# A long convolution with a gated block: late projections in the following second-stage stretch, taps from SBUF, ScalarE evacuating the last third stage, 120-row input tiles, warm-up matmuls

## The chip, the cores and the metric

One core of one Trainium2 chip runs the whole kernel. The metric is the device time of one execution in microseconds (us). Five engines work side by side: TensorE (PE, matmuls; its weight loads are listed as PEld), VectorE (DVE), ScalarE (ACT), GpSimd (POOL) and SyncE (SP), which here only issues the DMAs between HBM and SBUF. An instruction of one engine runs when those ahead of it on the same engine have run and the data and buffers that it names are ready.

## The reference

For every batch and channel, x is convolved causally with h over the whole sequence (a real FFT of twice the length), and the result y goes through a gated block. All is float32.

```python
B, S, D = 8, 6400, 128                       # x; h is [S, D]
y = irfft(rfft(x, n=2*S) * rfft(h, n=2*S))[:, :S, :]
gate = sigmoid(sum(conv_w[k] * shift(y, 4 - k) for k in range(5)))   # 5 taps along S
out = ((y @ w_val) * gate) @ w_out           # both weights 128 x 128
```

## The kernel before, in words

**Four stages.** The convolution of length 6400 is a transform written as matmuls with 6400 = 100 x 64. *First stage* (`Forward`): for each of 16 groups of 4 channels an x tile of 128 rows (two halves of 64 rows, 50 of each used) is loaded, POOL or DVE forms its sum and difference (`sums`, tile `sd`), 16 matmuls go into a pair of PSUM banks (`half`), and ScalarE copies the result into the large tile `gy`. *Second stage* (`s2_mm`): 13 blocks of 4 frequencies; each block is 16 matmuls with weights from a table `m2`, and a `Product` multiplies it by the spectrum of h: DVE reads PSUM twice (`mul_u` into `gy`, `mul_t` into the spectrum's own tile, named `h`), then POOL combines the two (`add`). *Third stage* (`s3_quads`, L330): 16 groups a batch, each into two PSUM banks, which ScalarE (`e[0]`) and VectorE (`e[1]`, L591) copy into the tile `dt`. *Fourth stage* (`Chunk.s4`): 13 chunks of up to five 100-long rows, with weights from `dt` and a table `m4_sb`.

**What follows a chunk.** `copies`: ScalarE copies the chunk's y from PSUM into SBUF and forms one or two scaled copies for the taps. `taps`: VectorE adds the others with scalar_tensor_tensor operations (`more`), which read y from PSUM, `self.p`; POOL adds one more. `project` is two matmuls of y with `w_val` into a PSUM bank, `sigm` the sigmoid on ScalarE, `gate` VectorE's product of the two, `output` two matmuls with `w_out`, `store` ScalarE's copy and SP's DMA to `out`. One projection or output takes one of four single banks (`ps1`), as a fourth stage and each bank of a third-stage group do. First-stage halves and products take pairs of banks (`ps2`, two pairs).

**Order of the work.** All instructions keep program order on their engine; each is recorded under one line (L98), that of the wrapper. The chunk with the sequence's last rows (`HEAD`, 4 rows at 60) is needed first, since the rows of one chunk continue in the next. Each of 8 batches has two parts. In the *third stage* the loop over `g` (L584) runs one third-stage group and one half of the next batch's first stage. In the *stretch* the loop over `s` (L611) runs the fourth stage of this batch's chunk `s` and the product `s + 1` of the next batch. Chunk `s - 2` is projected in step `s`, gated in the same step, and its output stands in step `s + 1`, behind the next Product, the next chunk's projection and the next fourth stage. Chunks that begin at row 35 or later (five of them, `late`) and `HEAD` are treated otherwise: their y stays in tiles `yl`, their gates in `gl`, and a list of steps (`trail`, L538) runs their taps, projection, sigmoid, gate, output and store inside the next batch's third stage, one step after each group. Their taps read the SBUF copy already. In the last batch nothing is late, and there is no next batch: its stretch holds only fourth stages and what follows a chunk (`finish`, L562).

**The start.** A *head* runs the first stage for h and for batch 0, and then (L513) the second stage for both: for each block the spectrum of h, its copy and its store to DRAM (`hd`), and batch 0's product. DVE also unpacks the block's float64 weights to float32 by 22 operations on bits (`weights`, L140), two in each of these steps. The fourth-stage table is loaded in 13 DMAs (L596) in batch 0's third stage, since its space holds other tiles before.

Of the kernel before, what the change touches and what calls it, by code (L numbers as in the profile page):

```python
# [16 lines left out]
C = 128  # L17
# [4 lines left out]
HP = 64  # L22
MW = 3 * HR
SB = 4
# [86 lines left out]
def longconv_moe(ctx: ExitStack, tc: tile.TileContext, x, h, r1, m2, r3, m4, w64, out):  # L111
# [98 lines left out]
    class Forward:  # L210
# [6 lines left out]
        def load(self, n=1):  # L217
            for _ in range(n):
                if self.n < NS:
                    nc.sync.dma_start(self.xs[self.n % len(self.xs)], self.src[self.n])  # L220
                    self.n += 1

        def sums(self, e):
            j = self.s
            if j >= NS:
                return
            self.s += 1
            x, sd = self.xs[j % len(self.xs)], sd_sb[(j + self.o) % 3]
# [141 lines left out]
    class Chunk:  # L370
# [33 lines left out]
        def copies(self):  # L404
            a, n = self.ch
            if a == HEAD[0]:
# [6 lines left out]
                return  # L413
            if self.late:
                act(self.y, self.p)
                self.p = self.y
                return
            self.init()
            act(self.y, self.p)
            self.q = p_t[a // CH % 2]  # L420
            self.first(3, self.q, self.p)
# [57 lines left out]
        def store(self):  # L479
            act(self.y, self.o)  # L480
            i, k = _out_range(self.ch)
            nc.sync.dma_start(out[self.b, i:k].rearrange("(e n t) -> e n t", e=C, n=self.ch[1]), self.y)
# [12 lines left out]
    nc.sync.dma_start(r1_sb, r1)  # L495
    fh.load(len(xh) - 1)
# [14 lines left out]
    nc.sync.dma_start(r3_sb, r3)  # L511
    sp, pr = {0: Spectrum(0)}, {}
    for kb in range(-1, NKB + 1):  # L513
# [8 lines left out]
        if 0 <= kb < NKB:  # L522
# [3 lines left out]
            next(wgen, None)  # L526
            next(wgen, None)
# [4 lines left out]
    class Gates:  # L532


        def __init__(self, b, defer):
            self.cs = [Chunk(b, ch, defer) for ch in CHUNKS]

        def trail(self):  # L538

            h, late = self.cs[0], [c for c in self.cs if c.late]  # L540
            steps = collections.defaultdict(list)
            for m, c in enumerate(late + [h]):
                t = 2 * m + 2
                if c is not h:
                    steps[t - 2].append(lambda c=c: c.taps(range(2)))
                    steps[t - 1].append(lambda c=c: c.taps(range(2, 4)))
                steps[t] += [c.project, c.sigm, c.gate]
                steps[t + 2].append(c.output)
                steps[t + 3].append(c.store)
            n = max(steps)  # L550
            return [lambda c=steps[i]: [f() for f in c] for i in range(n + 1)]

        def at(self, s, last):

            return self.cs[s] if 1 <= s < NCH else self.cs[0] if s == NCH and last else None

        def each(self, what, s, last=True):
            c = self.at(s, last)
            if c and not c.late:
                getattr(c, what)()  # L560

        def finish(self, s):  # L562
            self.each("project", s - 2)
            self.each("output", s - 3)
            self.each("store", s - 4)
            self.each("sigm", s - 2)
            if s == NCH:
                self.cs[NCH - 1].taps()
            self.each("gate", s - 2)

    trail = []
    fx = Forward(x[1], gy) if B > 1 else None
    if fx:
        fx.load(XB)
    for b in range(B):
# [3 lines left out]
        if trail:  # L579
            trail.pop(0)()  # L580
# [3 lines left out]
        for g in range(NS):  # L584
# [6 lines left out]
            e[1](dve)  # L591
            for u in f:
                u(act)
            if b == 0 and g < NKB:
                a = CH * g
                nc.sync.dma_start(m4_sb[:, a : a + CH], m4.rearrange("k (n t) -> k n t", t=MW)[:, a : a + CH])  # L596
# [6 lines left out]
            if trail:  # L603
                trail.pop(0)()
# [4 lines left out]
        gs = Gates(b, nxt)  # L609
        ps = {}  # L610
        for s in range(NCH):  # L611
            if s == 0:
                gs.cs[0].s4()
                gs.cs[0].copies()
                if nxt:
                    ps[0] = Product(0)
                    m2_load(M2B)
            if s == 1:
                gs.cs[s].s4()
# [3 lines left out]
            gs.each("project", s - 2)  # L623
            if s > 1:
                gs.cs[s].s4()
            gs.each("output", s - 3)
            gs.each("store", s - 4)
            gs.each("sigm", s - 2)
            if s:
                gs.cs[s].copies()  # L630
            if nxt:
                ps[s].mul_u()
            if s > 1 and not gs.cs[s - 1].late:
                gs.cs[s - 1].taps()
            if nxt:
                ps[s].mul_t()
                ps.pop(s).add()
                h_load(s + HB)
            if s == 0:
                gs.cs[0].taps()  # L640
            gs.each("gate", s - 2)
            if s == 10 and b + 2 < B:
                fx.load(XB)
        trail = gs.trail() if nxt else [lambda s=s: gs.finish(s) for s in range(NCH, NCH + 5)]
    for t in trail:
        t()
# [45 lines left out]
```

## Time and profile before

| | us |
|---|---|
| median of 3 runs (lowest to highest) | 1005.45 (1003.25 to 1007.77) |
| the profiled execution | 1006.82 |
| its span in the profile | 1005.0 |
| PE busy | 940.5 (94% of the span) |
| DVE busy | 702.8 (70%) |
| POOL busy | 544.5 (54%) |
| ACT busy | 475.5 (47%) |

The profile is of one execution; its times are read against its own 1006.82 us, of which the span is 1005.0. Busy time of PE is that of its matmuls, whose records overlap a little: where matmuls follow each other without a hole, the time from one start to the next is the price. In a row of a timeline stand the start, the duration, the engine, the line, the operation, what it writes and reads, its shape and the count; a bracket at the end is the time for which the engine had been idle, and what released it. `dt`, `yl` and `gl` with `w_sb` are projections and outputs, `gy` with `m` is a Product, `m_sb` with `dt` a fourth stage, `r_sb` with `gy` a third-stage group and `r_sb` with `sd` a first-stage half.

### The profile page before, as it was taken

How to read it: one execution, taken by the hardware profiler on the slowest of the kernel's cores; microseconds unless marked ns; L12 is line 12 of the kernel's file. 1: busy time of each engine (PE TensorE's matmuls, PEld its weight loads, DVE VectorE, ACT ScalarE, POOL GpSimd, SP SyncE). 2: the span in 40 equal slices, each digit the busy share in tenths (PEclk: the TensorE clock that was granted, in tenths of full speed). 3: DMA queues.
4: the chain of work that ended last, by engine and by line, in shares of the span. 5: the costliest groups of instructions: out<-in, count | busy, mean ns of one | idle time of the engine just before them, and what ended most of it. 6: DMA issues, size and time to landing. Idle time of an engine off the chain costs nothing.

```text
span 1005.0 us, 46982 instructions
## 1 busy us (share of the span) xinstructions
PE 940.5 (94%) x21360; PEld 793.5 (79%) x21360; DVE 702.8 (70%) x939; ACT 475.5 (47%) x916; POOL 544.5 (54%) x551
## 2 busy tenths in 40 slices
PE   7897778999999999999999998999989999999987
PEld 7797778787978878887878778887887878786753
DVE  5499217977398747977398756977399755978366
ACT  4521434445543653546444554445544553534465
POOL 6467434785277744785177743784367752760032
PEclk9898999999999999999999999999999999999989
DMA  7783854756467545755467555665467554750012
GB/s 253 244 272 149 283 204 158 225 157 194 134 229 214 156 154 194 230 159 166 150 223 218 153 159 186 216 176 170 145 211 221 151 178 159 229 140 34 31 42 91
DMA packets 96838, 177.33 MB, mean 176 GB/s; under 512 B 43392, under 2 KB 49792, under 8 KB 96640
## 3 DMA queue, kind: packets, MB, share of 16 engines
q1 hardware_dynamic: 96640, 174.34, 55.6%
q8 instruction: 167, 2.74, 1.1%
q14 instruction: 31, 0.25, 0.1%
HBM read 141.55 MB, written 32.77 MB: 173 GB/s over the span
## 4 chain that ended last, share of the span: by engine, by line
PE 90%; issue 5%; DVE 3%; POOL 1%; ACT 1%; DMA 0%; POOLq 0%; DVEq 0%; ACTq 0%
PE pt L98 90%; DVE gl L98 1%; DVE dt L98 1%; POOL gl L98 1%; ACT dt L98 1%; DVE gy L98 0%; POOL dt L98 0%; DMA x<-hl 0%; DVE sd L98 0%; DVE m_sb L98 0%; POOLq L688 0%; ACT gl L98 0%; ACT yl L98 0%; ACT gy L98 0%; DVEq L98 0%
## 5 line engine op out<-in xcount | busy, mean ns | idle before, releaser
L98 PE MATMUL pt<-r_sb,gy 64*64 64x128 f32 (+1 forms) x8192 | 267.3, 273 | 20.3 <-issue 11.5
L98 PEld LDWEIGHTS pt<-r_sb,gy 64*64 64x64 f32 (+1 forms) x8192 | 235.8, 130 | 63.8 <-ACT gl L98 20.4
L98 POOL TENSOR_TENSOR sd<-x 128x256 f32<-128x256 f32 x236 | 197.4, 860 | 154.2 <-issue 124.2
L98 POOL TENSOR_TENSOR gy<-gy,h 128x512 f32<-128x512 f32 (+1 forms) x182 | 221.6, 1241 | 63.6 <-DVE h L98 27.7
L98 ACT COPY dt<-pt 128x512 f32<-128x512 f32 (+3 forms) x269 | 155.2, 581 | 193.9 <-PE pt L98 191.6
L98 PEld LDWEIGHTS pt<-m_sb,dt 128*64 128x64 f32 x4096 | 191.5, 137 | 35.3 <-issue 22.7
L98 PEld LDWEIGHTS pt<-gy,m 128*64 128x64 f32 x3008 | 179.1, 135 | 43.8 <-issue 23.6
L98 PE MATMUL pt<-gy,m 128*64 128x128 f32 x3008 | 193.3, 278 | 17.5 <-issue 12.0
L98 PE MATMUL pt<-m_sb,dt 128*64 128x100 f32 x4096 | 198.0, 250 | 2.9 <-DVE dt L98 2.4
L98 DVE COPY dt<-pt 128x512 f32<-128x512 f32 (+1 forms) x136 | 92.5, 680 | 132.1 <-PE pt L98 125.6
L98 PE MATMUL pt<-r_sb,sd 50*64 50x100 f32 x4608 | 143.2, 258 | 17.2 <-issue 11.2
L98 DVE TENSOR_TENSOR gy<-pt,h 128x1024 f32<-128x1024 f32 (+1 forms) x99 | 116.8, 1180 | 46.3 <-PE pt L98 46.3
L98 DVE SCALAR_TENSOR_TENSOR gl<-yl,w_sb,gl 128x500 f32<-128x500 f32 x147 | 130.6, 892 | 24.6 <-ACT gl L98 22.1
L98 PEld LDWEIGHTS pt<-r_sb,sd 50*64 50x64 f32 x4608 | 128.9, 142 | 22.2 <-issue 14.5
L98 DVE SCALAR_TENSOR_TENSOR dt<-pt,w_sb,dt 128x500 f32<-128x500 f32 (+7 forms) x216 | 132.9, 631 | 13.5 <-POOL dt L98 3.8
L98 ACT COPY gy<-pt 128x400 f32<-128x400 f32 x248 | 110.2, 496 | 41.2 <-PE pt L98 32.8
L98 ACT ACTIVATE dt<-pt,w_sb 128x500 f32<-128x500 f32 (+1 forms) x64 | 40.0, 625 | 170.2 <-PE pt L98 169.4
L98 PE MATMUL pt<-dt,w_sb 128*64 128x500 f32 (+2 forms) x480 | 116.0, 561 | 0.8 <-DVE dt L98 0.4
L98 POOL TENSOR_TENSOR dt<-dt,p 128x500 f32<-128x500 f32 (+1 forms) x64 | 66.4, 1038 | 82.5 <-DVE dt L98 58.0
L98 DVE TENSOR_TENSOR h<-pt,h 128x1024 f32<-128x1024 f32 (+1 forms) x91 | 107.3, 1179 | 2.3
L98 ACT COPY yl<-pt 128x500 f32<-128x500 f32 (+1 forms) x96 | 54.5, 568 | 83.9 <-PE pt L98 83.9
L98 DVE TENSOR_TENSOR gl<-pt,gl 128x500 f32<-128x500 f32 (+1 forms) x48 | 31.7, 661 | 54.5 <-PE pt L98 50.8
(40 smaller groups left out, 568.5 us busy)
## 6 DMA issues: line engine op xcount, KB each, us to landing
m<-m SPq DMA_DIRECT2D x90, 512.0 KB, 4.7
h<-hd SPq DMA_DIRECT2D x84, 512.0 KB, 3.9
x<-xl SPq DMA_DIRECT2D x118, 256.0 KB, 3.4
out<-dt SPq DMA_DIRECT2D x56, 250.0 KB, 5.8
out<-yl SPq DMA_DIRECT2D x40, 250.0 KB, 2.5
m_sb<-m SPq DMA_DIRECT2D x13, 375.0 KB, 4.5
hd<-h SPq DMA_DIRECT2D x8, 512.0 KB, 5.1
m_sb<-m SPq DMA_DIRECT2D x6, 512.0 KB, 6.5
```

What stands on the lines that cost most here:

```text
L98: return self._tc.keep_in_program_order(call(*args, **kwargs))
```

## The change

1. **Late projections.** The list of steps is gone. In the third stage stay only the ten half-sets of late taps and two sigmoids. Projection, gate, output and store of `HEAD` and of the five late chunks (`pend`) go into the stretch that follows, in its steps 0, 0, 1, 1, 2 and 3 (`jobs`). A chunk of the batch's own is projected one step later than before (`i + 3`), and its output is the first PE work of the step after (`outs`), right behind its projection.
2. **Order on VectorE.** In a step `mul_u`, `mul_t`, the gate and the taps of the previous chunk follow each other; before it was `mul_u`, taps, `mul_t`, gate.
3. **Taps** read the SBUF copy of y in every chunk (`self.p = self.y`).
4. **Last third stage.** In the last batch ScalarE evacuates both banks of a group.
5. **Input tiles.** Loads, sums and differences cover 120 rows instead of 128 (`XR`).
6. **Warm-up.** VectorE zeroes a 128 x 128 tile, and seven matmuls of it run ahead of the first stage.
7. **The start's other work.** The weight unpacking moves from the head into batch 0's third stage, two operations a group; four of the 13 loads of the fourth-stage table move from there into steps 0 to 3 of the head's second stage.

*First place.* PE's order in two steps of batch 0's stretch, before. Names with `m4_sb` are fourth stages, those with `m2` Products; `dt` with `w_sb` is, behind a Product, the projection, and behind a fourth stage the output of the chunk before.

```order
L98 MATMUL pt1_2603<-m4_sb_68,dt_67 64x2x50 x20
L98 MATMUL pt1_2624<-dt_67,w_sb_71 64x500 x2
L98 MATMUL pt2_2643<-gy_66,m2_1_80 64x64x2 x16
L98 MATMUL pt1_2661<-dt_67,w_sb_71 64x500 x2
L98 MATMUL pt1_2664<-m4_sb_68,dt_67 64x2x50 x20
L98 MATMUL pt1_2685<-dt_67,w_sb_71 64x500 x2
L98 MATMUL pt2_2704<-gy_66,m2_2_81 64x64x2 x16
L98 MATMUL pt1_2722<-dt_67,w_sb_71 64x500 x2
```

After, the same place: projection and output of one chunk (`pt1_2747` and `pt1_2767`, `pt1_2809` and `pt1_2829`) stand next to each other, where a fourth stage stood between them, and the Product follows.

```order
L101 MATMUL pt1_2726<-m4_sb_68,dt_67 64x2x50 x20
L101 MATMUL pt1_2747<-dt_67,w_sb_71 64x500 x2
L101 MATMUL pt1_2767<-dt_67,w_sb_71 64x500 x2
L101 MATMUL pt2_2770<-gy_66,m2_0_79 64x64x2 x16
L101 MATMUL pt1_2788<-m4_sb_68,dt_67 64x2x50 x20
L101 MATMUL pt1_2809<-dt_67,w_sb_71 64x500 x2
L101 MATMUL pt1_2829<-dt_67,w_sb_71 64x500 x2
L101 MATMUL pt2_2832<-gy_66,m2_1_80 64x64x2 x16
```

What moved is the output: from a place five groups of matmuls behind its projection to the place right behind it.

*Second place.* VectorE's order in the same steps, before: the gate (`dt` from a bank and `dt`), `mul_u` (`gy`), three taps from a bank, `mul_t` (`h`).

```order
L98 TENSOR_TENSOR dt_67<-pt1_2661,dt_67 128x5x100
L98 TENSOR_TENSOR gy_66<-pt2_2643,h_3_85 128x2x64x8
L98 SCALAR_TENSOR_TENSOR dt_67<-pt1_2664,w_sb_71,dt_67 128x5x100 x3
L98 TENSOR_TENSOR h_3_85<-pt2_2643,h_3_85 128x1024
L98 TENSOR_TENSOR dt_67<-pt1_2722,dt_67 128x5x100
L98 TENSOR_TENSOR gy_66<-pt2_2704,h_0_82 128x2x64x8
```

After: both products stand ahead of the gate, the taps behind it, and their input is `dt` in SBUF.

```order
L101 TENSOR_TENSOR gy_66<-pt2_2647,h_3_85 128x2x64x8
L101 TENSOR_TENSOR h_3_85<-pt2_2647,h_3_85 128x1024
L101 TENSOR_TENSOR dt_67<-pt1_2747,dt_67 128x5x100
L101 SCALAR_TENSOR_TENSOR dt_67<-dt_67,w_sb_71 128x5x100 x3
L101 TENSOR_TENSOR gy_66<-pt2_2708,h_0_82 128x2x64x8
L101 TENSOR_TENSOR h_0_82<-pt2_2708,h_0_82 128x1024
L101 TENSOR_TENSOR dt_67<-pt1_2809,dt_67 128x5x100
```

The taps moved from between the two products to behind the gate, and from a bank to SBUF.

*Third place.* PE in the third stage of batch 1 before, between two groups (`r3_sb`), where late work stands: the output of one late chunk (`gl`) and the projection of the next (`yl`).

```order
L98 MATMUL pt1_3191<-r3_sb_70,gy_66 50x128 x2
L98 MATMUL pt2_3224<-r1_sb_69,sd_0_89 64x100 x16
L98 MATMUL pt1_3249<-gl_72,w_sb_71 64x500 x2
L98 MATMUL pt1_3252<-yl_40_75,w_sb_71 64x500 x2
L98 MATMUL pt1_3260<-r3_sb_70,gy_66 64x128 x2
```

After, none of these stands between groups; the first steps of the batch's stretch hold them, behind the last half of the first stage (`r1_sb`).

```order
L101 MATMUL pt2_3942<-r1_sb_69,sd_0_89 64x100 x16
L101 MATMUL pt1_3964<-yl_60_73,w_sb_71 64x400 x2
L101 MATMUL pt1_3968<-m4_sb_68,dt_67 64x2x50 x16
L101 MATMUL pt2_3985<-gy_66,m2_0_79 64x64x2 x16
L101 MATMUL pt1_4003<-gl_72,w_sb_71 64x400 x2
L101 MATMUL pt2_4008<-gy_66,m2_1_80 64x64x2 x16
L101 MATMUL pt1_4026<-yl_35_74,w_sb_71 64x500 x2
L101 MATMUL pt1_4039<-m4_sb_68,dt_67 64x2x50 x20
L101 MATMUL pt1_4060<-gl_72,w_sb_71 64x500 x2
L101 MATMUL pt2_4063<-gy_66,m2_2_81 64x64x2 x16
L101 MATMUL pt1_4081<-yl_40_75,w_sb_71 64x500 x2
L101 MATMUL pt1_4085<-yl_45_76,w_sb_71 64x500 x2
```

Twelve such groups a batch moved from between the third stage's groups into the stretch's first steps.

The diff, cut to what the prediction speaks of:

```diff
@@ sizes
+XR = 120
+WARM = 7
+M4H = 4
@@ Forward.load
-                    nc.sync.dma_start(self.xs[self.n % len(self.xs)], self.src[self.n])
+                    nc.sync.dma_start(self.xs[self.n % len(self.xs)][:XR], self.src[self.n, :XR])
@@ Forward.sums
-            x, sd = self.xs[j % len(self.xs)], sd_sb[(j + self.o) % 3]
+            x, sd = self.xs[j % len(self.xs)][:XR], sd_sb[(j + self.o) % 3][:XR]
@@ Chunk.copies
-                return
-            if self.late:
+            elif self.late:
                 act(self.y, self.p)
-                self.p = self.y
-                return
-            self.init()
-            act(self.y, self.p)
-            self.q = p_t[a // CH % 2]
-            self.first(3, self.q, self.p)
+            else:
+                act(self.y, self.p)
+                self.init()
+                self.q = p_t[a // CH % 2]
+                self.first(3, self.q, self.p)
+            self.p = self.y
@@ the start
+    warm = m2_sb[0][:, 0, 0]
+    nc.vector.memset(warm, 0.0)
+    pt = pair()
+    for _ in range(WARM):
+        nc.tensor.matmul(pt[:, 0, :C], lhsT=warm, rhs=warm, start=True, stop=True)
...
-            next(wgen, None)
-            next(wgen, None)
+        if 0 <= kb < M4H:
+            m4_load(kb)
@@ the third stage
+        late = [lambda c=c, j=j: c.taps(range(j, j + 2)) for c in pend[1:] for j in (0, 2)]
+        late += [c.sigm for c in pend[:2]]
...
-            e[1](dve)
+            e[1](dve if nxt else act)
...
+            if b == 0:
+                next(wgen, None)
+                next(wgen, None)
+                if g + M4H < NKB:
+                    m4_load(g + M4H)
...
-            if trail:
-                trail.pop(0)()
+            if late:
+                late.pop(0)()
@@ the stretch, after
+        for i, c in enumerate(pend):
+            jobs[(0, 0, 1, 1, 2, 3)[i]].append(c)
+        for i, c in enumerate(cs):
+            if i and not c.late:
+                jobs[i + 3 if i < 9 else i + 2].append(c)
+        if not nxt:
+            jobs[NCH + 1].append(cs[0])
+        ps, outs = {}, []
+        for s in range(max([NCH - 1, *jobs]) + 2):
+            todo = list(jobs[s])
+            if s == 0 and pend:
+                todo.pop(0)
+                pend[0].project()
+                pend[0].gate()
+            if s < 2:
+                cs[s].s4()
+            if nxt and s == 0:
+                ps[0] = Product(0)
+                m2_load(M2B)
+            for c in outs:
+                c.output()
+            if s == 0 and pend:
+                pend[0].output()
+                pend[0].store(p_t[1][:, : HEAD[1]])
+            if nxt and s + 1 < NKB:
+                ps[s + 1] = Product(s + 1)
+                m2_load(s + 1 + M2B)
+            if 1 < s < NCH:
+                cs[s].s4()
+            for c in todo:
+                c.project()
+                if c not in pend[:2]:
+                    c.sigm()
+            for c in outs:
+                c.store()
+            if s < NCH:
+                cs[s].copies()
+            if s in ps:
+                ps[s].mul_u()
+                ps[s].mul_t()
+                ps.pop(s).add()
+                h_load(s + HB)
+            for c in todo:
+                c.gate()
+            if 0 < s <= NCH and not cs[s - 1].late:
+                cs[s - 1].taps()
+            outs = todo
...
+        pend = [cs[0]] + [c for c in cs if c.late]
```

More of the change, by code (lines that the diff above doesn't have):

```diff
@@ L477, in output, with store @@
                     )
-        def store(self):
-            act(self.y, self.o)
+        def store(self, y=None):
+            y = self.y if y is None else y
+            act(y, self.o)
             i, k = _out_range(self.ch)
-            nc.sync.dma_start(out[self.b, i:k].rearrange("(e n t) -> e n t", e=C, n=self.ch[1]), self.y)
+            nc.sync.dma_start(out[self.b, i:k].rearrange("(e n t) -> e n t", e=C, n=self.ch[1]), y)
     wgen = weights()
@@ L511, in longconv_moe, with m4_load @@
     nc.sync.dma_start(r3_sb, r3)
+    def m4_load(j):
+        a = slice(CH * j, CH * j + CH)
+        nc.sync.dma_start(m4_sb[:, a], m4.rearrange("k (n t) -> k n t", t=MW)[:, a])
     sp, pr = {0: Spectrum(0)}, {}
@@ L530, in longconv_moe @@
     ps1 = ctx.enter_context(tc.tile_pool(name="ps1", bufs=4, space=bass.MemoryType.PSUM))
[L532 to L571, printed above, removed]
     fx = Forward(x[1], gy) if B > 1 else None
@@ L574, in longconv_moe @@
         fx.load(XB)
+    pend = []
     for b in range(B):
         nxt = b + 1 < B
-        if trail:
-            trail.pop(0)()
+        late = [lambda c=c, j=j: c.taps(range(j, j + 2)) for c in pend[1:] for j in (0, 2)]
+        late += [c.sigm for c in pend[:2]]
         if nxt:
@@ L590, in longconv_moe @@
             e[0](act)
-            e[1](dve)
+            e[1](dve if nxt else act)
             for u in f:
                 u(act)
-            if b == 0 and g < NKB:
-                a = CH * g
-                nc.sync.dma_start(m4_sb[:, a : a + CH], m4.rearrange("k (n t) -> k n t", t=MW)[:, a : a + CH])
+            if b == 0:
[3 more added lines that the diff above has]
+                    m4_load(g + M4H)
             if nxt and g % 2 and g > 1:
@@ L602, in longconv_moe @@
                     h_load(kb - M2B)
-            if trail:
-                trail.pop(0)()
+            if late:
+                late.pop(0)()
         if b + 2 < B:
             fx = Forward(x[b + 2], gy)
[L609 to L619, printed above, removed]
+        cs = [Chunk(b, ch, nxt) for ch in CHUNKS]
+        jobs = collections.defaultdict(list)
+        for i, c in enumerate(pend):
[22 more added lines that the diff above has]
+                pend[0].store(p_t[1][:, : HEAD[1]])
             if nxt and s + 1 < NKB:
@@ L622, in longconv_moe @@
                 m2_load(s + 1 + M2B)
[L623 to L631, printed above, removed]
+            if 1 < s < NCH:
[9 more added lines that the diff above has]
+            if s in ps:
                 ps[s].mul_u()
-            if s > 1 and not gs.cs[s - 1].late:
-                gs.cs[s - 1].taps()
-            if nxt:
                 ps[s].mul_t()
@@ L638, in longconv_moe @@
                 h_load(s + HB)
-            if s == 0:
-                gs.cs[0].taps()
-            gs.each("gate", s - 2)
+            for c in todo:
[3 more added lines that the diff above has]
+            outs = todo
             if s == 10 and b + 2 < B:
                 fx.load(XB)
-        trail = gs.trail() if nxt else [lambda s=s: gs.finish(s) for s in range(NCH, NCH + 5)]
-    for t in trail:
-        t()
+        pend = [cs[0]] + [c for c in cs if c.late]
 def _lay_x(v):
```

## The prediction

> **What bounds the kernel now.** The page first: the engines' shares and the chain that ended last.
>
> ```profile
> PE 940.5 (94%) x21360; PEld 793.5 (79%) x21360; DVE 702.8 (70%) x939; ACT 475.5 (47%) x916; POOL 544.5 (54%) x551
> PE 90%; issue 5%; DVE 3%; POOL 1%; ACT 1%; DMA 0%; POOLq 0%; DVEq 0%; ACTq 0%
> ```
>
> TensorE (PE) is the bound, with a tenth of the span elsewhere. The busy table by stage (width, then busy time of PE, PEld, DVE, ACT, POOL, granted clock, DMA share, GB/s) shows where. Its rows are the third stage of batch 0, the third stage and the stretch of batch 2, all of batches 1 to 6, then the third stage and the last stretch of batch 7.
>
> ```profile
> 97.10:154.60 57.50, 45.23 (x1537) 42.42 (x1537) 12.23 (x17) 22.70 (x46) 23.68 (x33) 0.94 0.62 213
> 328.50:381.50 53.00, 52.73 (x1588) 43.22 (x1585) 32.55 (x43) 32.00 (x64) 27.13 (x32) 1.00 0.49 155
> 381.50:441.90 60.40, 57.90 (x978) 50.24 (x976) 51.09 (x67) 24.19 (x46) 40.92 (x37) 1.00 0.71 211
> 214.90:900.80 685.90, 664.22 (x15339) 559.52 (x15336) 502.59 (x654) 337.09 (x660) 407.41 (x408) 1.00 0.59 182
> 900.80:946.90 46.10, 42.79 (x1075) 31.72 (x1072) 28.59 (x43) 18.66 (x34) 0.00 (x0) 1.00 0.10 35
> 946.90:1005.00 58.10, 49.12 (x620) 31.28 (x620) 37.68 (x63) 35.82 (x67) 15.45 (x15) 0.94 0.20 58
> ```
>
> In the middle PE is busy 97%: there a step removed from PE is worth its time and a wait put on PE costs its time. Six stretches of 60.4 taken from 685.9 leave 54.0 per third stage of batches 1 to 6. Idle PE lies in batch 0 (12.3 us) and at the end (9.0 us). PE's and DVE's timelines in a steady step of the stretch:
>
> ```profile
> 295.31 1.01 PE L98 MATMUL pt<-dt,w_sb 128*64 128x500 f32 x4
> 296.15 1.89 PE L98 MATMUL pt<-m_sb,dt 128*64 128x100 f32 x40
> 297.87 1.01 PE L98 MATMUL pt<-dt,w_sb 128*64 128x500 f32 x4
> 298.70 2.01 PE L98 MATMUL pt<-gy,m 128*64 128x128 f32 x32
> 300.54 1.01 PE L98 MATMUL pt<-dt,w_sb 128*64 128x500 f32 x4
> ...
> 298.90 1.22 DVE L98 TENSOR_TENSOR gy<-pt,h 128x1024 f32<-128x1024 f32 x1
> 300.04 2.28 DVE L98 SCALAR_TENSOR_TENSOR dt<-pt,w_sb,dt 128x500 f32<-128x500 f32 x3
> 302.23 1.22 DVE L98 TENSOR_TENSOR h<-pt,h 128x1024 f32<-128x1024 f32 x1
> 303.36 0.67 DVE L98 TENSOR_TENSOR dt<-pt,dt 128x500 f32<-128x500 f32 x1
> ```
>
> From start to start, output 0.84, fourth stage 1.72, projection 0.84 and Product 1.84 make 5.24 us without a hole. DVE's loop is 5.13 (1.14 + 2.19 + 1.13 + 0.67).
>
> **The change part by part.** *Late projections.* In batches 1 to 6 six projections and six outputs (12 × 0.84 = 10.1 us) leave the third stage. What a quad group then takes is seen where none stood, at the start of batch 0's third stage:
>
> ```profile
> 97.11 0.70 PE L98 MATMUL pt<-r_sb,gy 64*64 64x128 f32 x8 [5.24 <-DVE gy L98]
> 98.51 2.92 PE L98 MATMUL pt<-r_sb,gy 64*50 64x128 f32 x56 [0.70 <-DVE gy L98]
> ...
> 101.94 1.93 PE L98 MATMUL pt<-r_sb,gy 64*64 64x128 f32 x64
> 103.69 0.87 PE L98 MATMUL pt<-r_sb,sd 50*64 50x100 f32 x32
> 104.38 1.83 PE L98 MATMUL pt<-r_sb,gy 64*64 64x128 f32 x60
> ```
>
> Quads 1.75 and Forward 0.69 are 2.44 us, 16 of them 39.0. The late taps stay, on DVE; groups by form of two third stages (batch 7 without Forward, batch 2 with POOL's sums), and DVE's and ACT's quad copies of batch 7:
>
> ```profile
> L98 DVE SCALAR_TENSOR_TENSOR gl<-yl,w_sb,gl 128x500 f32<-128x500 f32 x20 | 14.7, 737 | 3.5 <-ACT gl L98 3.2
> L98 DVE COPY dt<-pt 128x512 f32<-128x512 f32 x16 | 11.0, 688 | 10.9 <-PE pt L98 10.9
> ...
> L98 ACT COPY dt<-pt 128x512 f32<-128x512 f32 x16 | 9.4, 586 | 25.8 <-PE pt L98 25.0 <-ACT gl L98 0.8
> ```
> ```profile
> L98 DVE SCALAR_TENSOR_TENSOR gl<-yl,w_sb,gl 128x500 f32<-128x500 f32 x20 | 18.6, 930 | 3.5 <-ACT gl L98 3.1
> ```
>
> One copy and two taps are 0.69 + 2 × 0.93 = 2.55 us for ten groups: 1.1 over PE's pitch. With 0.9 of entry I take 41.0, so −13.0 a batch. Bounds: 40 (no contention), 42.2 (the excess of 0.19 a tap grows by 54/41).
>
> In the stretch the 12 come back: +9.7 (the head's two are a fifth shorter, 2 × 0.84 × 0.2). Early steps have two holes that they fill, −2.5:
>
> ```profile
> 392.21 2.08 PE L98 MATMUL pt<-gy,m 128*64 128x128 f32 x32 [1.73 <-issue]
> ...
> 396.79 2.07 PE L98 MATMUL pt<-gy,m 128*64 128x128 f32 x32 [0.78 <-PE pt L98]
> ```
>
> *The new wait.* An output now follows its own projection on PE with the gate between; before, a Product or a fourth stage stood there. Behind the waiting output, in PE's order, stand the next Product and fourth stage, so nothing covers it. Its price from late-projection and end-of-kernel rows:
>
> ```profile
> 922.91 1.01 PE L98 MATMUL pt<-yl,w_sb 128*64 128x500 f32 x4
> ...
> 924.03 0.68 DVE L98 TENSOR_TENSOR gl<-pt,gl 128x500 f32<-128x500 f32 x1 [1.21 <-PE pt L98]
> ```
> ```profile
> 996.97 0.67 DVE L98 TENSOR_TENSOR gl<-pt,gl 128x500 f32<-128x500 f32 x1
> ...
> 997.79 1.06 PE L98 MATMUL pt<-gl,w_sb 128*64 128x500 f32 x4 [1.66 <-DVE gl L98]
> ```
>
> Projection to gate 1.12, gate 0.68, gate end to output 0.15, less the projection's 0.84: 1.1 us. DVE must be free then: gate 0.67, three taps and two products (2.27) are 5.2 to 6.0 us (taps at 0.74 or 1.01) in a step of 6.34, so it is. The six stores that move along stand on SP's queue behind the outputs' ACT copies, and a spectrum load behind each; loads are issued three to four steps ahead, 19 us or more, and 1.5 MB at 211 GB/s (7 us) fit into the idle 0.29 of the DMA engines (17 us): nothing, at worst the loads' lead. Per batch 1 to 6, ten waits of full length less the one that the fourth stage covers, and 0.3 for the step with two: 9 × 1.1 + 0.3 = 10.2.
>
> *Taps from SBUF.* Beside POOL with two SBUF inputs a tap took 0.93 us, alone 0.74; the stretch's own taps, read from PSUM, 0.73 (2.19 for three). Most of the excess is hidden behind the wait above; it shows in the first steps, where DVE is late already (the 0.78): five head pieces × 0.19, +1.0 a stretch, bounds 0 to 4. [...]
>
> So a batch 1 to 6 gets −13.0 + 9.7 − 2.5 + 10.2 + 1.0 = **+5.4, six times +32.4**. Batch 0's stretch has no late work: seven waits and the taps, 7.7 + 1.0 = **+8.7**.
>
> *Batch 7, third stage:* without the late work two quads are 1.75; ACT's two copies (1.17) and half a late initial tap fit in that. 16 × 1.75 + 0.5 = 28.5: **−17.6**. ACT instead of DVE alone costs nothing while it stays under 1.75; DVE, with taps only, has 14.7 of 28. *Last stretch:* steps 0 to 3 with moved work 17.1; seven steps of 1.72 + 0.84 + 1.1 + 0.84 = 4.5, 31.5; two with step 11's double job 9.8; the tail 2.8 + 3.6 + 2.0; the last copy and store 2.5. That is 69.3, **+11.2**; the chain of taps and POOL add that ran there before is the rival to a step of 4.5, and shorter (3.7 between like rows at 982.32 and 986.04, below).
>
> ```profile
> 982.32 1.26 POOL L98 TENSOR_TENSOR gl<-gl,p 128x500 f32<-128x500 f32 x1 [2.47 <-ACT gl L98]
> ...
> 986.04 1.25 POOL L98 TENSOR_TENSOR gl<-gl,p 128x500 f32<-128x500 f32 x1 [2.46 <-DVE gl L98]
> ```
>
> *Start.* The first stage and the head's second stage (last row) by the table:
>
> ```profile
> 0.00:4.00 4.00, 0.08 (x1) 0.08 (x2) 0.42 (x1) 1.28 (x1) 0.72 (x5) 1.00 0.52 160
> 4.00:13.20 9.20, 9.20 (x221) 8.61 (x224) 4.05 (x10) 3.53 (x8) 6.66 (x9) 1.00 0.96 344
> 13.20:17.00 3.80, 3.74 (x137) 3.12 (x130) 3.80 (x8) 3.02 (x8) 3.80 (x5) 1.00 0.74 222
> 17.00:44.30 27.30, 20.75 (x636) 19.28 (x633) 16.37 (x30) 13.71 (x31) 15.47 (x20) 0.81 0.82 257
> 44.30:92.00 47.70, 47.56 (x847) 47.18 (x846) 40.87 (x45) 14.13 (x16) 26.66 (x21) 1.00 0.68 226
> ```
>
> A matmul takes 42 ns until 13.2 and 28 after: 3.1 us too much. Warm-up in the 3 idle us can take away all of it, or, if 9.2 us of work must pass first, 3 × (1 − 28/42) = 1. I take **−2** (0 to −3). [...] *Weight unpacking* leaves the head's DVE queue, which PE waits for at its end (5.24 + 0.70); a block has two products (2.3 together) and two unpacking steps there, and with some 2 us of these gone it is to about 3.7: **−2.2** (0 to −4). It moves under batch 0's third stage, where DVE has 45 us free (12.2 of 57.5 busy). *That third stage* takes 16.5 more than the 41.0 of one without late work; four of 13 fourth-stage table loads go ahead of it, and x tiles are a sixteenth smaller: 4/13 × 16.5 = 5, and some 2 of the x bytes, **−7** (−2 to −16.5). Four loads in the head meet a DMA share of 0.68 and hide there.
>
> Sum: −2 − 2.2 − 7 + 8.7 + 32.4 − 17.6 + 11.2 = +23.5 on the profiled execution's 1006.82, whose span is 1005.0; that is 1030.3, and on the median, 1.4 lower, **1029 us**.
>
> **Rivals.** *First, the early stops go altogether (not slower).* In the first 155 us PE loses 3.9 + 6.6 idle and 6.2 in slow matmuls (42 against 28 ns; 636 records at 33) before 44.3, 5.2 at the head's end, 16.5 in batch 0's third stage: 38.4. If the stops come from full DMA queues and the shifted loads and smaller tiles undo all of it, −38.4 takes the place of −11.2: 1002 us. For it: DMA at 0.62 to 0.96 there. Against: only four loads move, in 13.2 to 44.3 the loads stay. It beats the waits only if over 34.7 of the 38.4 go (the other terms). Chance 0.17, 0.10 of it faster by over 0.5%.
> [...] POOL's two halves of a product's add:
>
> ```profile
> L98 POOL TENSOR_TENSOR gy<-gy,h 128x512 f32<-128x512 f32 x24 | 30.3, 1284 | 9.2 <-DVE h L98 4.6 <-issue 2.3 <-PE pt L98 2.2
> ```
>
> Taps now come right after both products, when these run. If each excludes the other, DVE's loop is 2.27 + 2.19 + 2 × 1.28 = 7.0, against 6.34: 0.7 us in six steps less the 1.0 counted, 3 us × 7 batches, +21: 1050. Against: 0.93 on average. Chance 0.15.
> *Third, a cheaper gate wait*, because DVE starts the gate sooner than at 924.03, where it had waited: at 0.7 us, 72 waits (54 + 7 + 11) return 29: 1000. Break-even is 23.5/72 below 1.1, at 0.78. Against: the gate alone is 0.68. Chance 0.11, 0.07 of it faster.
>
> **How the numbers follow.** The forecast has 0.57, own range 1012 to 1042. 0.5% is about what a measurement of this kernel can tell from no change. Faster 0.10 + 0.07 = 0.17; same 0.07 + 0.04 = 0.11; slower 0.57 + 0.15 = 0.72. The range 994 to 1048 leaves out the edges of the first and third rival (0.05), half of the second (0.07) and the forecast's tails (0.05).
>
> **What would show it.** Right: third stages of about 41 us, a stretch of 78 to 79 with a hole of 1.1 us on PE ahead of each output, released by DVE's gate; batch 7 at 28.5 and 69. Wrong: holes under 0.8 us, third stages over 43, taps of 1.3 us or more in the stretch, or a first 155 us shorter by 30.

## The result, and the profile after

The changed kernel takes 1131.17 us (median of 4 runs, 1126.96 to 1132.11), the kernel before 1004.86 beside it: a ratio of 1.1245, 95% interval 1.1206 to 1.1285. The forecast was 1029 with a range to 1048, so the direction was right and the size was not: 126 us were lost where 24 were forecast.

The page of the changed kernel, its shares and its chain:

```profile
PE 952.6 (84%) x21374; PEld 795.2 (70%) x21374; DVE 762.8 (68%) x924; ACT 488.3 (43%) x932; POOL 563.1 (50%) x551
PE 61%; DVE 25%; issue 10%; POOL 2%; ACT 1%; DMA 0%; SPq 0%; POOLq 0%; DVEq 0%
```

PE is busy for 12 us more, in a span 123.5 us longer. On the chain VectorE has 25% where it had 3%, and "issue", time in which the engine waits for nothing that the profile shows, 10% where it had 5%. The table by stage: third stage and stretch of batch 0, of batch 2, third stage and last stretch of batch 7, then all of batches 1 to 6.

```profile
99.80:159.50 59.70, 46.12 (x1536) 43.64 (x1536) 21.37 (x39) 22.73 (x46) 24.40 (x33) 0.92 0.57 176
159.50:235.00 75.50, 62.22 (x973) 51.76 (x972) 64.37 (x67) 26.38 (x48) 43.17 (x36) 0.95 0.52 161
366.35:418.35 52.00, 43.42 (x1540) 40.96 (x1542) 29.00 (x37) 27.30 (x56) 27.26 (x33) 0.97 0.44 136
418.35:497.20 78.85, 68.22 (x1018) 51.78 (x1014) 64.76 (x72) 29.55 (x56) 42.81 (x36) 1.00 0.57 172
1023.60:1053.30 29.70, 29.45 (x1028) 28.44 (x1029) 15.26 (x21) 20.89 (x40) 0.63 (x1) 1.00 0.02 4
1053.30:1128.50 75.20, 58.74 (x666) 33.59 (x663) 41.12 (x68) 41.23 (x78) 15.53 (x15) 0.95 0.21 65
...
235.00:1023.60 788.60, 670.89 (x15337) 556.89 (x15337) 563.99 (x654) 341.26 (x661) 423.83 (x410) 0.99 0.52 156
```

Six stretches of 78.9 taken from 788.6 leave 52.5 for a third stage of batches 1 to 6. From the same boundaries in both traces:

| part | before | after | change | forecast |
|---|---|---|---|---|
| to batch 0's third stage | 97.1 | 99.9 | +2.8 | −4.2 |
| batch 0, third stage | 57.5 | 59.7 | +2.2 | −7 |
| batch 0, stretch | 60.3 | 75.5 | +15.2 | +8.7 |
| batches 1 to 6, third stages | 324 | 315 | −9 | −78 |
| batches 1 to 6, stretches | 362 | 474 | +111 | +110 |
| batch 7, third stage | 46.1 | 29.7 | −16.4 | −17.6 |
| batch 7, last stretch | 58.1 | 75.2 | +17.1 | +11.2 |

PE's steady step in a stretch of the changed kernel (projection, output, Product, fourth stage):

```profile
455.48 1.01 PE L101 MATMUL pt<-dt,w_sb 128*64 128x500 f32 x4
457.92 1.06 PE L101 MATMUL pt<-dt,w_sb 128*64 128x500 f32 x4 [1.44 <-DVE dt L101]
458.78 2.05 PE L101 MATMUL pt<-gy,m 128*64 128x128 f32 x32
460.62 1.93 PE L101 MATMUL pt<-m_sb,dt 128*64 128x100 f32 x40
462.33 1.05 PE L101 MATMUL pt<-dt,w_sb 128*64 128x500 f32 x4
464.61 1.06 PE L101 MATMUL pt<-dt,w_sb 128*64 128x500 f32 x4 [1.22 <-DVE dt L101]
```

A step is 6.85 us from projection to projection (455.48 to 462.33); the output waits 1.2 to 1.4 us, released by the gate. VectorE in the same step:

```profile
454.71 1.22 DVE L101 TENSOR_TENSOR gy<-pt,h 128x1024 f32<-128x1024 f32 x1
455.96 1.23 DVE L101 TENSOR_TENSOR h<-pt,h 128x1024 f32<-128x1024 f32 x1
457.11 0.67 DVE L101 TENSOR_TENSOR dt<-pt,dt 128x500 f32<-128x500 f32 x1
457.69 3.88 DVE L101 SCALAR_TENSOR_TENSOR dt<-dt,w_sb 128x500 f32<-128x500 f32 x3
461.49 1.22 DVE L101 TENSOR_TENSOR gy<-pt,h 128x1024 f32<-128x1024 f32 x1
```

It has no hole: from one first product to the next are 6.78 us (454.71 to 461.49). VectorE sets the step, and the three taps take 3.88 us where they took 2.28. PE in the third stage, where a row with "issue" interrupts a group whose buffers and data are there:

```profile
382.65 0.52 PE L101 MATMUL pt<-r_sb,sd 50*64 50x100 f32 x15
384.64 0.64 PE L101 MATMUL pt<-r_sb,sd 50*64 50x100 f32 x17 [1.46 <-issue]
...
403.20 1.36 PE L101 MATMUL pt<-r_sb,gy 64*64 64x128 f32 x41
...
407.48 1.31 PE L101 MATMUL pt<-r_sb,gy 64*50 64x128 f32 x18 [2.93 <-issue]
```

One half of the first stage is cut in two, 15 and 17 of its 32 records, and stands 1.46 us between; no semaphore lies inside it. So two things were to be explained: VectorE's taps, and a third stage that lost 12 late matmul pairs and hardly became shorter.

### The profile page after: what moved, and what is told of

It reads as the page before. It is cut to its first block, busy times and chain, and to the rows that moved or that the text cites. A ratio compares the mean times of both kernels' runs of the same rounds, so it can differ in the third digit from the quotient of the medians.

```text
span 1128.5 us, 46938 instructions
## 1 busy us (share of the span) xinstructions
PE 952.6 (84%) x21374; PEld 795.2 (70%) x21374; DVE 762.8 (68%) x924; ACT 488.3 (43%) x932; POOL 563.1 (50%) x551
## 4 chain that ended last, share of the span: by engine, by line
PE 61%; DVE 25%; issue 10%; POOL 2%; ACT 1%; DMA 0%; SPq 0%; POOLq 0%; DVEq 0%
PE pt L101 61%; DVE dt L101 16%; DVE gy L101 4%; DVE h L101 2%; DVE gl L101 2%; POOL gy L101 2%; DMA m_sb<-hl 0%; ACT dt L101 0%; ACT p L101 0%; DVE sd L101 0%; POOL gl L101 0%; SPq L101 0%; ACT gl L101 0%; DVE m_sb L101 0%; POOLq L678 0%
## 5 line engine op out<-in xcount | busy, mean ns | idle before, releaser
L101 ACT COPY dt<-pt 128x512 f32<-128x512 f32 (+3 forms) x285 | 163.1, 582 | 386.3 <-PE pt L101 357.1
L101 PE MATMUL pt<-r_sb,gy 64*50 64x128 f32 (+1 forms) x8192 | 277.2, 276 | 51.7 <-issue 43.8
L101 POOL TENSOR_TENSOR gy<-gy,h 128x512 f32<-128x512 f32 (+1 forms) x182 | 239.2, 1338 | 163.3 <-PE pt L101 122.2
L101 PEld LDWEIGHTS pt<-r_sb,gy 64*50 64x50 f32 (+1 forms) x8192 | 246.1, 133 | 64.3 <-issue 51.3
L101 POOL TENSOR_TENSOR sd<-x 120x256 f32<-120x256 f32 x236 | 196.9, 858 | 144.7 <-issue 113.7
L101 DVE SCALAR_TENSOR_TENSOR dt<-dt,w_sb 128x500 f32<-128x500 f32 (+2 forms) x192 | 190.3, 1007 | 3.2
L101 DVE COPY dt<-pt 128x512 f32<-128x512 f32 (+1 forms) x120 | 81.5, 679 | 159.9 <-PE pt L101 125.6
L101 DVE SCALAR_TENSOR_TENSOR gl<-yl,w_sb,gl 128x500 f32<-128x500 f32 (+2 forms) x187 | 155.0, 832 | 41.1 <-ACT gl L101 28.6
L101 PE MATMUL pt<-r_sb,sd 50*64 50x100 f32 x4608 | 153.8, 261 | 31.4 <-issue 28.7
L101 PEld LDWEIGHTS pt<-dt,w_sb 128*64 128x64 f32 x480 | 27.5, 137 | 116.7 <-DVE dt L101 76.2
```

The source lines that it names most:

```text
L101: return self._tc.keep_in_program_order(call(*args, **kwargs))
```

## The experiments

Each kernel ran on the chip beside the kernel before (medians of 1003.4 to 1005.0 us, single runs of 1001.7 to 1008.5). Only the start's edits (nine runs) and the last batch alone (six) were run more than once, so a few us between two of the others tell nothing. "Stretch" and "third stage" are those of batches 1 to 6 if no batch is named.

**Outputs later.** The gate wait's cover is put back.

```diff
-            for c in outs:
-                c.output()
             if s == 0 and pend:
                 pend[0].output()
...
             if 1 < s < NCH:
                 cs[s].s4()
+            for c in outs:
+                c.output()
             for c in todo:
                 c.project()
```

> The changed kernel with the outputs behind the next Product and fourth stage, so that PE no longer stands between a projection and its own output. Theory (VectorE's loop sets the step, because the taps from SBUF meet POOL's adds): the step stays at 6.8 us, a stretch of batches 1 to 6 at 77 to 79 us, the whole within 10 us of 1131. Rival (the gate wait of 1.1 us sets the step): the step falls to 5.3 us, a stretch to 68 to 70, the whole to about 1050.

Measured: 1115.83 us, stretch 78.3, batch 0's 74.6, last stretch 68.8. PE's timeline:

```profile
455.55 2.06 PE L101 MATMUL pt<-gy,m 128*64 128x128 f32 x32 [1.32 <-DVE h L101]
457.44 1.89 PE L101 MATMUL pt<-m_sb,dt 128*64 128x100 f32 x40
459.16 1.84 PE L101 MATMUL pt<-dt,w_sb 128*64 128x500 f32 x8
462.35 2.06 PE L101 MATMUL pt<-gy,m 128*64 128x128 f32 x32 [1.34 <-DVE h L101]
```

The step is still 6.80. PE's hole moved from the output to the Product, whose pair of banks VectorE has not yet emptied. The gate wait is not what sets the step. In the last stretch, which has no Products, its removal gave 6.4 us; with 0.6 in each of the six stretches it makes 10 of the 15.3 by which the whole fell, for at most 10 by the theory.

**No POOL adds.** The Products' adds on POOL are left out in the stretches.

```diff
-                ps.pop(s).add()
+                ps.pop(s)
```

> The changed kernel with POOL's adds of the Products left out in the stretches (part of the second stage is not computed). Theory (taps and POOL's adds exclude each other): a tap falls from 1.24 to about 0.74 us, VectorE's loop to 5.2, and the gate wait of 1.1 us alone sets a step of about 6.3 us; a stretch of batches 1 to 6 falls from 78.9 to about 75. Rival (a tap with two SBUF inputs is slow by itself in this place): taps stay at 1.2 us and a stretch at 78 to 79.

Measured: 1108.79 us, stretch 76.1, batch 0's 66.7. The taps' group in batch 2's stretch, by form, first in the changed kernel and then here:

```profile
L101 DVE SCALAR_TENSOR_TENSOR dt<-dt,w_sb 128x500 f32<-128x500 f32 x16 | 19.8, 1240 | 0.4
```
```profile
L101 DVE SCALAR_TENSOR_TENSOR dt<-dt,w_sb 128x500 f32<-128x500 f32 x16 | 11.8, 736 | 0.4
```

The same operations on the same SBUF operands take 0.736 us without POOL's adds, and from PSUM, in the same stretch of the kernel before, 0.737: their place in SBUF costs nothing by itself here. The timeline of the changed kernel, in short windows that part the taps (one, two, three of them), shows how they meet POOL's two adds:

```profile
457.32 1.27 POOL L101 TENSOR_TENSOR gy<-gy,h 128x512 f32<-128x512 f32 x1 [1.10 <-PE pt L101]
457.69 1.44 DVE L101 SCALAR_TENSOR_TENSOR dt<-dt,w_sb 128x500 f32<-128x500 f32 x1
...
457.69 3.11 DVE L101 SCALAR_TENSOR_TENSOR dt<-dt,w_sb 128x500 f32<-128x500 f32 x2
458.55 1.72 POOL L101 TENSOR_TENSOR gy<-gy,h 128x512 f32<-128x512 f32 x1
```

POOL's first add ends at 458.59, the first tap 0.54 later, at 459.13; the second add ends 1.14 after that, at 460.27 instead of the 459.82 that its usual 1.27 would give; the second tap ends 0.53 after it, at 460.80; the third, alone, takes 0.77. Behind the end of the other, each operation still needs most of its own time (0.54 and 0.53 of 0.74, 1.14 of 1.27): they take turns. What makes them do so, no run shows.

**Both.** The last two edits together.

> The changed kernel with both: outputs behind the next Product and fourth stage, and POOL's product adds left out (part of the second stage is not computed). Theory (gate wait and exclusion lie over each other, so that either alone keeps most of the loss): a stretch of batches 1 to 6 falls from 78.9 to 68 to 69, while either alone gave 78.3 and 76.1; the step is 5.3 us. Rival (something third holds the step): 75 or more.

Measured: 1039.96 us. Batch 2's stretch:

```profile
394.10:462.00 67.90, 66.78 (x1018) 51.92 (x1014) 55.41 (x72) 28.18 (x55) 10.26 (x12) 1.00 0.66 196
```

78.9 us fall to 68.0 (batch 0's 75.5 to 60.4), while one edit alone leaves 78.3 or 76.1. The two waits lie over each other: of the 10.9 us the gate wait, left alone, keeps 8.1, and the taps' turns with POOL, left alone, keep 10.3.

**Late work alone.** The changed kernel with the early chunks' taps from PSUM, between the two products, and outputs later (the diff shows the taps). Edits 4 to 7 of the change, and the projection one step later, stay in.

```diff
-            self.p = self.y
+            if self.late:
+                self.p = self.y
...
                 ps[s].mul_u()
+            if 0 < s <= NCH and not cs[s - 1].late:
+                cs[s - 1].taps()
+            if s in ps:
                 ps[s].mul_t()
...
-            if 0 < s <= NCH and not cs[s - 1].late:
-                cs[s - 1].taps()
```

> The changed kernel with three things put back: taps from PSUM, taps between the two products, outputs behind the next Product and fourth stage. So the late work alone is moved. Theory: a third stage stays at 52 to 54 us, a stretch of batches 1 to 6 is 60.4 + 9.7 - 2.5 = 67.6, batch 0's stretch 60.3, and the whole is 1035 to 1045: slower than before by what the third stage does not give back. By the prediction's 41 us third stage it would be about 965.

Measured: 1039.84 us. Its stretch of batch 2, third stage and last stretch of batch 7:

```profile
392.60:461.00 68.40, 66.74 (x1018) 51.86 (x1014) 54.88 (x72) 28.71 (x56) 39.94 (x36) 1.00 0.67 199
945.90:975.20 29.30, 29.02 (x1028) 28.11 (x1028) 15.26 (x21) 20.35 (x39) 0.68 (x1) 1.00 0.02 5
975.20:1038.10 62.90, 56.10 (x666) 33.49 (x664) 41.15 (x68) 40.70 (x78) 15.42 (x15) 1.00 0.25 77
```

The moved work costs a stretch 8.1 us (68.5 against 60.4; forecast 7.2), and the third stages, 50.9 to 54.4, give back 1.6 of it on average. In batch 7 the same move, with ScalarE's copies, gains: 92.1 against 104.2. Step by step from the changed kernel, the outputs' place is worth 15 us (1131.17 to 1115.83), the taps' source and place 76 (to 1039.84), and some 35 over the kernel before are left (in the profiles 39 in batches 1 to 6, 6 ahead of them, −12 in batch 7).

**Taps from SBUF alone**, on the kernel before.

```diff
             self.first(3, self.q, self.p)
+            self.p = self.y
```

> The kernel before with one edit: the taps of the early chunks read the SBUF copy. Here gate and first product stand between the second product and the taps, so that POOL's first add runs beside operations that read PSUM. Theory (exclusion of taps and POOL's adds): the first tap or two still meet the second add, taps take 0.9 to 1.1 us on average, VectorE's loop is 5.7 to 6.2 us and a stretch 63 to 67 us; the whole 1025 to 1050. Rival (an operation with two SBUF inputs costs the same here as from PSUM): 1005.

Measured: 1051.07 us, stretch 66.9, a tap 1.06 us on average (x16), the step 6.13. In the order of before, gate and first product run beside POOL's first add, so that the taps meet the second alone. This one edit costs 46 us; the whole is 1 us over the range of the theory.

**Long matmuls put in.** A projection's worth of PE work in 12 groups of each third stage.

```diff
+            if nxt and b and g < 12:
+                fill = single()
+                for k in range(2):
+                    nc.tensor.matmul(fill[k * HP : (k + 1) * HP, : CH * N1], lhsT=w_sb[:, k * HP : (k + 1) * HP],
+                                     rhs=yl[35], start=True, stop=True)
```

> The changed kernel with 12 additional pairs of long matmuls (a projection each, its result not used) between the groups of each third stage of batches 1 to 6: 10.1 us more PE work a batch. Theory (the third stage is paced by the supply of PE's instructions, and long matmuls give it time): a third stage stays at 52 to 54 us, the whole at 1131 to 1143. Rival (PE's work plus waits for buffers pace it): a third stage grows to about 62, the whole to about 1190.

Measured: 1145.80 us, third stages of 54.2 to 56.6 where the changed kernel has 51.5 to 54.6. Batch 2's third stage and PE's waits in it, here:

```profile
367.60:422.90 55.30, 54.64 (x1588) 42.35 (x1590) 29.14 (x37) 27.25 (x56) 27.91 (x33) 1.00 0.41 128
```
```profile
PE pt L101 <- issue: 0.4, 2, 0.3
```

In the changed kernel the same row of the waits reads:

```profile
PE pt L101 <- issue: 8.3, 6, 2.9
```

10.1 us of matmuls cost 2.5, as the stops went; the third stage, 55.0 on average, and the whole lie a little over the theory's ranges and far under the rival's 62 and 1190. This is how the kernel before hid its late work: its own row in batch 2's third stage reads

```profile
PE pt L98 <- issue: 0.3, 1, 0.3
```

**Short matmuls put in.** The same columns, in 20 matmuls of 50 instead of 2 of 500.

```diff
-                    nc.tensor.matmul(fill[k * HP : (k + 1) * HP, : CH * N1], ..., rhs=yl[35])
+                    for j in range(0, CH * N1, 50):
+                        nc.tensor.matmul(fill[k * HP : (k + 1) * HP, j : j + 50], ..., rhs=y35[:, j : j + 50])
```

> As the run with 12 additional pairs of long matmuls in each third stage, but each pair cut into 20 matmuls of 50 columns: about the same columns for PE, 432 more instruction records (matmuls with their weight loads) a third stage. Theory (the supply of PE's instructions paces the third stage, near 60 records a us): 7 us more than with the long ones, 60 to 64 us a third stage. Rival (PE's own work paces it): 55 to 57, as with the long ones.

Measured: 1237.15 us, third stages of 69.6 to 71.0. This run does not tell the theories apart. A matmul and its weight load have two records each here, so that 72 more stand in a group, 864 in a stage, twice the number expected; and a group's 40 matmul records took 2.27 us:

```profile
400.19 2.34 PE L101 MATMUL pt<-yl,w_sb 128*64 128x50 f32 x40
402.46 1.98 PE L101 MATMUL pt<-r_sb,gy 64*64 64x128 f32 x64
```

At 57 ns a record PE was slow by itself, and busy 70.08 of 70.6 us. Of stops there was next to nothing.

**No x loads** in the third stages (13 of 16 a batch), and **no transfers there**, which leaves out the table loads as well.

```diff
                 if self.n < NS:
+                  if self.n < XB or len(self.xs) > XB:
                     nc.sync.dma_start(...)
...
-            if nxt and g % 2 and g > 1:     # the second kernel only
+            if False:
```

> The changed kernel with 13 of the 16 x loads of each batch from 1 on left out (the first stage reads old tiles, so its input is wrong); the loads of Product and spectrum tables stay. Theory (PE's stops come each 255 instructions, when the next block of its instructions lands late behind data transfers): with half of the data gone the stops shrink and a third stage of batches 1 to 6 falls from 52 to 42 to 47 us. Rival (the stops are PE's own, whatever moves): it stays at 52. By the other rival (the chain of x load, POOL sum and first stage) it falls to 41.

> The changed kernel without 13 of 16 x loads a batch and without the table loads in the third stage (first and second stage read old data). Theory in the form that the run without x loads left (PE's instructions are supplied at some 66 records a us at best, and data transfers make it worse): a third stage of batches 1 to 6 takes 46 to 48 us, with stops of about 0.6 us each 255 records. Rival (transfers alone make the stops): 41 us and no stops.

Measured: 1098.96 and 1075.65 us; third stages of 47.4 to 49.8 and of 44.0 to 46.9 (batch 0: 51.4 and 47.8, for 59.7). Batch 2's third stage and PE's waits, without x loads:

```profile
353.80:402.30 48.50, 42.79 (x1540) 39.65 (x1542) 28.94 (x37) 27.28 (x56) 26.50 (x33) 1.00 0.20 74
```
```profile
PE pt L101 <- issue: 5.5, 9, 1.5
```

Without any:

```profile
347.20:391.80 44.60, 42.57 (x1542) 39.84 (x1544) 28.67 (x37) 27.30 (x56) 28.61 (x33) 1.00 0.02 5
```
```profile
PE pt L101 <- issue: 1.7, 4, 0.5
```

Data transfers make 7.1 of the 11.5 us by which the changed kernel's third stage exceeds 41.0. With none, some stops of 0.5 us are left. Leaving out the x loads shrank less than the theory said (48.6 on average for 42 to 47), leaving out all of them rather more (45.4 for 46 to 48), and no rival came out. A part may be the clock: the granted share in batch 2's third stage was 0.97 in the changed kernel and 1.00 in these two, and PE was busy there for 43.42 us against 42.79 and 42.57.

Where the stops fall tells what they are. PE's records (matmuls and weight loads) counted from the program's first, at each hole of over 0.35 us in batch 0's third stage:

```
before  4230 4485 4739 4994 5249 5504 5758 6013 6268
after   4228 4483 4738 4992      5502 5756 6011 6266
```

They lie 254 or 255 records apart, in both kernels at the same numbers within 2, though the warm-up puts 28 more records ahead of all work in the changed one: the holes keep to the count of instructions, and fall at other places of the work. With PE's semaphore instructions, which the trace holds too, the spacing is 256: every hole of the list stands at 193 or 194 of 256 in that count. So do all 48 holes of over 0.55 us in the changed kernel's third stages of batches 0 to 6 (their first 2 us left out), and the long ones of the head's first stage (1.77, 2.09 and 1.85 us at 34.4, 40.8 and 47.0). The queue of instruction transfers in batch 2's third stage:

```profile
q8 instruction: 12, 0.20, 1.5%
```

Twelve blocks of 16 KB for 3082 records, 257 each. At the longest hole of this stage (404.28 to 407.48) such a block was under way from 404.99 to 406.03. At the pace of 192 records of quads and first-stage halves in 2.44 us (79 a us), PE runs through 257 records in 3.25 us; the transfers of this stage's blocks began 3.5 to 6.6 us apart.

What ends a hole tells it more directly. All 48 holes end 1.2 to 1.6 us after a block has landed (1.45 at the longest: 406.03 to 407.48), and so do the 72 over 0.55 us in the runs without x loads and without any. A block's own transfer hardly changes: 0.9 to 1.6 us, median 1.09, with all data, and 0.9 to 1.4, median 1.05, without. What data change is when it starts: 1.3 to 2.1 us before the hole without any, and anywhere from 2.2 before to 1.5 after with them.

**The start's edits alone**, on the kernel before: 120 rows, warm-up, unpacking and four table loads moved.

```diff
+XR = 120
+WARM = 7
+M4H = 4
...
@@ the head
-            next(wgen, None)
-            next(wgen, None)
+        if 0 <= kb < M4H:
+            m4_load(kb)
...
@@ batch 0's third stage
+                next(wgen, None)
+                next(wgen, None)
...
```

> The kernel before with the edits of the start alone: 120-row tiles, warm-up, weight unpacking in batch 0's third stage, four table loads in the head. By the prediction's terms it gains 11 us: third stage of batch 0 starts 4 us earlier (93) and takes 50. By the theory that stops at the start and in that third stage are late instruction blocks of PE, which these edits don't touch: the third stage starts at 97 to 101 and takes 57 to 60, and the whole is within 5 us of the kernel before.

Measured: 1008.32 us, a ratio of 1.0042, interval 1.0016 to 1.0067. Batch 0's third stage starts at 100.5 in the profiled execution, which was 6 us longer than the median:

```profile
100.50:159.50 59.00, 45.88 (x1537) 43.30 (x1537) 20.79 (x39) 22.69 (x46) 24.27 (x33) 0.92 0.58 178
```
```profile
PE pt L101 <- issue: 12.4, 9, 3.3
```

The edits lose a little. The stops, 11.0 us before and 12.6 in the changed kernel, are still there with nine of the table loads and smaller tiles.

**ScalarE's evacuation alone**, on the kernel before.

```diff
-            e[1](dve)
+            e[1](dve if nxt else act)
```

> The kernel before with the one edit that ScalarE evacuates both banks in the last third stage. Theory (late projections and taps, not the copies, pace that stage): 44 to 47 us where it was 46.1, the whole 1002 to 1006. Rival (VectorE's copies hold the taps there): 40 us, the whole about 999.

Measured: 1004.26 us beside a median of 1004.09; the third stage 46.0 (46.1 before). Nothing by itself: the copies do not pace that stage while late work stands in it. Whether VectorE's copies would, once it is gone, was not run.

**The last batch alone.** The kernel before, and in batch 7 the order of the run with the late work alone (late work in the last stretch, taps from PSUM, outputs behind the fourth stage, ScalarE's evacuation).

```diff
+        if not nxt:
+            cs = [Chunk(b, ch, nxt) for ch in CHUNKS]
...
-        trail = gs.trail() if nxt else [lambda s=s: gs.finish(s) for s in range(NCH, NCH + 5)]
...
+        trail = gs.trail()
+        if b + 2 == B:
+            pend = [gs.cs[0]] + [c for c in gs.cs if c.late]
+            trail = [lambda c=c, j=j: c.taps(range(j, j + 2)) for c in pend[1:] for j in (0, 2)]
+            trail += [c.sigm for c in pend[:2]]
```

> The kernel before for batches 0 to 6; in the last batch alone the late projections go into the final stretch and ScalarE evacuates the third stage, with taps from PSUM and outputs behind the next fourth stage. There is no first stage and hardly a transfer in that third stage, so that its PE work is worth its time. Theory: third stage 29.3 us (46.1 before) and final stretch 62.8 (58.1 before), 12 us less: 993 us, ratio 0.988. Rival (the stages before hide or give back the gain): 1005.

Measured: 995.69 us against 1004.09, a ratio of 0.992, interval 0.9895 to 0.9945. Third stage and last stretch of batch 7:

```profile
897.50:926.40 28.90, 28.90 (x1031) 28.26 (x1030) 15.25 (x21) 21.07 (x40) 0.00 (x0) 1.00 0.02 5
926.40:989.20 62.80, 55.99 (x666) 33.42 (x664) 41.15 (x68) 40.55 (x78) 15.44 (x15) 1.00 0.25 77
```

91.7 us stand where 104.2 stood, 12.5 less in the profile, which is of the shortest of its six runs; the medians differ by 8.4 for the 12 of the theory. It beats both kernels, the one before by 0.8%.

## Why the prediction was wrong, step by step

*Third stages, −13.0 each: the step that failed.* 41.0 us came from three groups at the start of batch 0's third stage, where PE ran without a stop, times 16. A group at that pace uses 192 records in 2.44 us, and no third stage of the kernel before but batch 0's asked PE for so many over so long: there late work was absent, and it took 57.5. I read that excess of 16.5 us as the price of the table loads and x bytes around it. It was the sample of what each third stage becomes without late work: 52.5, −1.5 for −13.0. Six times the difference is 69 us, most of the miss. The late matmuls were the cover under which instructions arrived (in batch 2's third stage PE's "issue" waits came to 0.3 us with them, in the kernel before, and to 8.3 in the changed one); the wait for instruction blocks was a term that the sum did not have.

*The stretches, +18.4 each, measured +18.6.* The sum came out right by luck, by way of another mechanism. Nine gate waits of 1.1 us a stretch were to set a step of 6.34, and taps at 0.93 to hide behind them. In fact VectorE's loop sets it, at 6.78. The second rival (the taps and POOL's adds exclude each other), at 0.15, had the mechanism, with 7.0 for that loop; its 1050 fell short because the third stages were wrong in it too. The signs that were to show the forecast right, a stretch of 78 to 79 and a hole of 1.1 us or so ahead of each output, released by the gate, came out as well, so they could not tell the two apart; the runs without adds and with later outputs do. What hid it is, I think, the average of 0.93 from the third stage, where POOL's operations are short (0.88 on average) and leave holes, so that the same taking of turns looks mild; no run tests that. The price of the gate wait was about right where it is seen alone: without POOL's adds a step takes 6.37 us (projections at 448.76 and 455.13), and the stretch is 76.1, 8.1 above the 68.0 without either, for nine waits of 1.1 less what other work still covers. In batch 0's stretch the same swap of cause costs 15.2 for 8.7; two stops of PE of 4.3 us in all stand there too.

*Batch 7.* Third stage −16.4 for −17.6. Last stretch +17.1 for +11.2: the step came out as priced (outputs at 1080.19 and 1084.64, 4.45 for 4.5); the rest was the tail, 27.0 us from step 11 on for 20.7, where outputs of the last chunks waited up to 3.0 us for their gates. By the runs, taken in this order, 6.4 of the 17.1 are the outputs' place (75.2 to 68.8), 6.0 the taps' source and place (to 62.8), which the sum had at nothing here, and 4.7 the moved work.

*Start, gap and batch 0's third stage, −11.2, measured +5.* The head's end gap shrank as forecast (3.41 us for 5.24 ahead of the next matmul), and the first six halves took 6.7 us for 8.7, the 2 us forecast for the warm-up, which no run has alone. Then PE stood for 2.65 us at 12.0, where it had gone on before: its next instruction block was under way from 12.10 to 13.24, before from 10.42 to 11.38. Behind that stop the granted clock was 0.50 from 14.4 to 21.2, where the kernel before had 1.00 from 12.2 to 19.0, and it was 0.68 over the head's first pair of blocks, which took 5.3 us instead of 3.7 at 1.00. The third stage kept its stops. By the run of these edits alone the kernel loses 0.2 to 0.7%. Why that block came later, and which of the edits is to blame, was not settled.

*The first rival* (early stops go) named the right hole and the wrong cure: in batch 0's third stage the excess shrinks with the transfers (59.7 to 51.4 and 47.8 in the two runs without them), and the edits moved too few. The stops of the head were not tried.

## What to carry to other kernels

Before work is taken from a stage because PE is 97% busy there, look for a stretch of the same trace in which that work is already absent, and take its whole length, not the pitch of its first groups. Here PE went through 79 records a us with matmuls of 100 and 128 columns, and long matmuls put among them hid in the stops (10.1 us cost 2.5). When an operation gets its second input from SBUF, look at what POOL does at that moment, operation by operation; an average from another stage hides it (0.93 us a tap in the third stage before, 1.24 in the stretch after). Two waits that lie over each other must be removed together.

## What the runs showed of the hardware

PE's stops in the third stages stand 254 or 255 matmuls and weight loads apart, or a multiple of that, at the same place of every 256 of its instructions (193 or 194); where PE ran without one, it went through up to 79 records a us. Beside data transfers a stop took 0.4 to 3.9 us from start to start in the changed kernel; in batch 2's third stage the longest left PE idle for 2.93 us, and without transfers for 0.5. All 48 stops of over 0.55 us in the changed kernel ended 1.2 to 1.6 us after a 16 KB block of instructions had landed. At 73 records a us with no data on their way (128 in 1.75 us, batch 7's third stage, PE busy for 29.45 of 29.70 us), and at 57 a us beside them (4042 records in 70.6 us, the run with short matmuls, PE busy for 70.08), there were practically no stops. In a steady step of the changed kernel a tap of 0.74 us took 1.44 to 1.64 beside an add of POOL, and the second of the two adds 1.72 instead of 1.27. A block's own transfer took 1.09 us (median) with all data and 1.05 without; its start lay up to 1.5 us behind the start of the hole with them, and 1.3 us or more ahead of it without. Whether a block is asked for late or waits behind data, the traces don't show.
